# Early expert weights in an attention and mixture-of-experts kernel: five staging buffers, a step moved to the end of a tick, and one matmul group a tick later

## The chip, the cores and the metric

The kernel runs on one core of a Trainium2 chip. The metric is device time in microseconds (us) of one execution; lower is better. Durations of single instructions come from one profiled execution of the kernel before.

## What is computed

Two stages follow each other, and the second needs the first.

```python
# attention: batch 4, heads 8, 768 positions, head size 64, blocks of 32 positions
mask = |block_i - block_j| <= 1, or first or last block, or one of 3 sampled blocks per query block
attn = softmax(where(mask, q @ k.T / 8, -1e9));  x = (attn @ v) as [3072 tokens, 512]
# mixture of experts: 8 experts, hidden size 1024, one expert per token
logits = x @ w_gate + modality_bias[modality_id];  e = argmax(logits);  g = softmax(logits)[e]
out[token] = g * (relu(x @ w1[e]) @ w2[e])
```

## The kernel before, in words

**Attention.** Tokens are handled in 24 tiles of 128. Each half of the batch gives one "dense" tile (first and last block, against all keys) and 11 sparse tiles m = 0 to 10; over both halves the sparse tiles are g = 0 to 21. A sparse tile is four items. For each item the program runs steps named by a letter: S scores (L537), M masked maximum (L545, VectorE), X exponential (L553, ScalarE), T transposes (L562, TensorE), A copy of the transposes out of PSUM (L567, ScalarE); and for each tile W, the product with the values that both query blocks share (`weigh_shared`, L584), V, the product with the values that each has for itself (`weigh_own`, L593), O the division (L447), Y a turn of the tile (L600, L602) and G the gate (L610). The values lie in two buffers, one for even and one for odd g, which are filled anew for each tile: `fetch_v` (L499, L500), `fetch_own` (L525, six transfers of 128 KB), all in the queue of SyncE, and `share_v` (L507, GpSimd), which copies rows from the tile before.

**The order of the work.** It is written out by hand. The loop over ticks t emits in each tick the steps in the order `ORDER` = O X T S M G V A Y W, each for the item that lies `LAG` ticks back, and between them it calls `hook(0)` to `hook(7)`: hook 0 before O, 1 before X, 2 before T, 3 before S, 4 before M, 5 before A, 6 before W, 7 behind all steps. A hook runs the loads put at that place, and by `ADVANCE`, `CHOOSE` and `EARLY` one or more pieces of three generators: the routing of finished tiles, the choosers, and the early groups. There are NI = 104 items; from tick NI on the generators are stepped at the end of each tick, twice in a tick. Every engine's own queue keeps the order in which the program emits.

**The early groups.** `choose(0)` (from 16 finished tiles) and `choose(1)` (from 18) each pick an expert with enough tokens already, so that group 0 and group 1 of 256 tokens can start before attention ends. `choose` multiplies a one-hot matrix on TensorE (L1100, 16 or 18 matmuls of two columns) to get token numbers. `early_groups` (L816) is stepped once per tick. While attention runs, its inner `load(nf, ns)` fetches weight pieces up to nf and splits them up to ns: `fetch` (L712) issues one transfer of 512 KB on SyncE's queue into a staging buffer (`staged`, L709; L720 for pieces of w1, L724 for w2), and `split` (L726) rounds the piece to a high part (a cast on ScalarE, L731) and subtracts to get the low part (L737: on VectorE, or for the pieces in `POOL_SPLITS`, 1, 2, 4 and others, in four parts on GpSimd). The parts go into a ring of NRING buffer pairs `wh`, `wl`. Eight pieces make one expert. `column` (L774, L778, L779) turns the gathered tokens of a group. At the tail (tick NI + 7) the last buffers are set up, and the matmuls of group 0 begin: `up` (L785 to L787), `relu` (L792, L793), `down` (L800 to L802), with `load` calls by the tables `DOWN0`, `UP1`, `DOWN1`.

**Buffers.** SBUF is cut into ten slots, used first by attention and then by the experts (`expert_slots`, L665). Before, the first eight pieces have only two staging buffers in slot 4 (and, for piece 7, one in slot 7, which is free only at the tail), in the order 0, 1, 0, 1, 0, 1, 0, 2; from piece 8 on there are five. The guard in `load` counts with NSTG = 5 all the same, so the transfer of piece 2 is issued when piece 0 is split and has to wait in SyncE's queue until that split has read its buffer. The first tick of the early groups is t = NI - 13, so tick k of `TICKS` is t = NI - 13 + k up to k = 12; ticks 13 and 14 are both at the end of t = NI, 15 and 16 at the end of NI + 1.

**The rest.** From 10 more groups on (`first_layer`, `second_layer`, `later`) the same steps run with LOOK_D = 6 pieces of fetch and LOOK_S = 4 pieces of split ahead.

Of the kernel before, what the change touches and what calls it, by code (L numbers as in the profile page):

```python
# [9 lines left out]
F32 = mybir.dt.float32  # L10
F32R = mybir.dt.float32r
# [51 lines left out]
LHS = (6, 5)  # L63
LHS_DVE = (True, True)
CHOOSE = ((0, 2),)
EARLY = ((3, 3),)

KL = (0, 3)
QP = (-2, 2)
# [10 lines left out]
EVAC_DVE = ()  # L80
POOL_SPLITS = (1, 2, 4, 7, 15, 16, 21)

TICKS = (6, 9, 12)
DOWN0 = ((9, 5), (9, 7), (14, 7), (12, 9), (13, 9), (13, 9), (17, 9), (15, 10))
UP1 = ((13, 8), (13, 14), (17, 15), (20, 15))
DOWN1 = ((16, 17), (17, 16), (17, 17), (23, 18), (21, 17), (23, 18), (23, 19), (22, 19))
# [3 lines left out]
def attention_moe(ctx, tc, kD, qD, qH, v0, v1, blocks, modality, w_gate, bias, w1, w2, out):  # L90
# [33 lines left out]
    with ExitStack() as actx:  # L124
# [5 lines left out]
        def bank():  # L130
            return psum.tile([P, 512], F32, name="bank")


        def slot(n, dt=F32):
            return big.tile([P, 3 * 1024 + (16 if n == 8 else 0)], dt, name="slot", tag=f"slot{n}", bufs=1)
# [521 lines left out]
        stg, wh, wl, xg, xh, xl, hh, hl, og, xq = [], [], [], [], [], [], [], [], [], []  # L657

        def pieces(n, dt, *sizes):
            t, k = slot(n, dt), 0  # L660
            for size in sizes:
                yield t[:, k:k + size]
                k += size

        def expert_slots(*ns):  # L665
            cols_ = lambda ap: ap.rearrange("p (c t) -> p c t", t=GT)
            W, X = 1024, HD
            for n in ns:
                if n == 0:
                    w = [*pieces(1, F32R, W, W, W), *pieces(3, F32R, W, W, W)]  # L670
                    wh[:], wl[:] = w[0::2], w[1::2]
                    wx = list(pieces(9, F32R, W - 16, W, W))[1:]
                    xh.append(cols_(wx[0]))
                    xl.append(cols_(wx[1]))
                    a = list(pieces(4, F32, W, W, X, X))
                    stg.extend(a[0:2])
                    xg.extend(a[2:4])
                elif n == 2:
                    w = [*pieces(0, F32R, W, W, W), *pieces(2, F32R, W)]
                    wh.extend(w[0::2])  # L680
                    wl.extend(w[1::2])
                elif n == 5:
                    a = list(pieces(5, F32R, 2 * W, W))
                    hh.append(cols_(a[0]))
                    hl.append(cols_(a[1]))
                elif n == 6:
                    a = list(pieces(6, F32R, W, W, W))
                    hl.append(cols_(a[0]))
                    xh.append(cols_(a[1]))
                    xl.append(cols_(a[2]))  # L690
                elif n == 7:
                    stg.extend(pieces(7, F32, W, W, W))
                elif n == 8:
                    a = list(pieces(8, F32, X, X, X, X, W))
                    xg.extend(a[0:2])
                    og.extend(a[2:4])
                    xq.append(a[4].rearrange("p (j f) -> p j f", f=P))

        NSTG, NRING, LOOK_D, LOOK_S = 5, 5, 6, 4
        experts = {}  # L700
        out_t = dram_disjoint_views(out, 2)

# [4 lines left out]
            return experts[g]  # L707

        def staged(n):  # L709
            return stg[(0, 1, 0, 1, 0, 1, 0, 2)[n] if n < 8 else n % NSTG]  # L710

        def fetch(n):  # L712
            g, c = divmod(n, 8)
# [12 lines left out]
        def split(n):  # L726
            split_high(n)
            split_low(n, nc.gpsimd if n in POOL_SPLITS else nc.vector)

        def split_high(n):  # L730
            nc.scalar.copy(wh[n % NRING], staged(n))  # L731
# [84 lines left out]
        def early_groups():  # L816
            now = {"fetch": 0, "split": 0, "gather": 0, "column": 0}

            def load(nf, ns):
                while True:  # L820
                    f, p = now["fetch"], now["split"]
                    if p < ns and p < f:
                        split(p)
                        now["split"] += 1
                    elif f < nf and f - NSTG < p and (f < 8 * NEAR or known):
                        fetch(f)
                        now["fetch"] += 1
                    else:
                        return

            def rows(g):
                if now["gather"] == g and ready[g] and (g != 1 or tail[1]):
                    if g == 1:
                        expert_slots(8)
                    gather(g)
                    now["gather"] += 1

            def columns(g):
                for n in range(2):
                    if now["column"] == 2 * g + n and now["gather"] > g:  # L840
                        column(g, n, bank())
                        now["column"] += 1
                        return

            expert_slots(0)
            tick, wait = 0, 0
            while not tail[0]:
                rows(0)
                if now["gather"]:
                    wait += 1  # L850
                    if wait > 4:
                        columns(0)
                p = sum(tick >= x for x in TICKS)
                load(p + 2, p)
                tick += 1
                yield "tick"
            expert_slots(2, 5, 6, 7)
            while now["column"] < 2:
                rows(0)
                columns(0)  # L860
# [186 lines left out]
        def choose(i):  # L1047
            n = TES[i]
# [46 lines left out]
            while any(t < n for t in slots_todo):  # L1095
                yield "tick"
            yield "tick"
            tp = bank()
            for t in range(n):
                nc.tensor.matmul(tp[:, 0:2], lhsT=lhs[:, t, :], rhs=hoh[:, t, :], start=t == 0, stop=t == n - 1)  # L1100
# [120 lines left out]
        def hook(place):  # L1221
            for f in work_at.pop((t, place), []):
                f()
            if t < NI:
# [4 lines left out]
                for at_, k in CHOOSE:  # L1229
                    if place == at_:  # L1230
                        step(choosers, k)
                for at_, k in EARLY:
                    if place == at_:
# [220 lines left out]
```

## Time and profile before

| | |
|---|---|
| device time, median of 3 runs | 520.99 us (517.85 to 523.48) |
| the profiled execution's own time | 519.21 us |
| its span in the trace | 517.4 us |
| mean granted TensorE clock in it | 0.995 of full |
| TensorE busy | 496.7 us, 96% of the span |
| VectorE, ScalarE, GpSimd busy | 389.6, 338.9, 295.1 us |
| moved by DMA | 119.40 MB |

Time outside the span is 519.21 - 517.4 = 1.8 us. PE is TensorE's matmuls, PEld its weight loads, DVE VectorE, ACT ScalarE, POOL GpSimd, SPq the queue of SyncE. Attention runs to about 227 us, and behind it only the experts. A matmul's end is modelled, so a busy PE can hide short stalls; its idle time can't.

### The profile page before, as it was taken

The numbers are of one execution on the slowest core, as the hardware profiler recorded it, in microseconds if no ns is written. First come the engines' busy times: TensorE is split into PE (matmuls) and PEld (weight loads), VectorE is DVE, ScalarE is ACT, GpSimd is POOL, SyncE is SP. The second block draws the span as 40 slices with busy tenths as digits, with TensorE's granted clock in tenths as the row PEclk, the third lists the DMA queues.
The fourth block names the chain that finished last, engine by engine and source line by source line (L and its number), as shares of the span: only waits on it lengthen the run. The fifth ranks groups of instructions, "written<-read, shape, count | busy, mean of one in ns | idle before, by whom it ended". The sixth has DMA issues, their size and how long they took to land.

```text
span 517.4 us, 18858 instructions
## 1 busy us (share of the span) xinstructions
PE 496.7 (96%) x7170; PEld 419.2 (81%) x7170; DVE 389.6 (75%) x1127; ACT 338.9 (66%) x777; POOL 295.1 (57%) x530
## 2 busy tenths in 40 slices
PE   8999989999999989889999999999999999999994
PEld 6677766777777767779989898989989899898983
DVE  7986788677689899866976669586785867759572
ACT  3799877998889988944554456464564546646471
POOL 3579775667458875752457624563845648465410
PEclk9999999999999999899999999999999999999999
DMA  8998788878956787656867875857749567595760
GB/s 281 326 243 232 223 226 250 240 208 249 253 161 186 205 265 224 184 179 243 275 227 252 316 254 158 308 184 264 270 164 333 174 241 249 195 343 157 262 202 23
DMA packets 49698, 119.40 MB, mean 231 GB/s; under 512 B 8512, under 2 KB 8896, under 8 KB 49600
## 3 DMA queue, kind: packets, MB, share of 16 engines
q1 hardware_dynamic: 44656, 105.00, 64.4%
q0 software_dynamic: 4944, 13.11, 7.0%
q8 instruction: 58, 0.95, 0.8%
q14 instruction: 40, 0.33, 0.2%
HBM read 105.50 MB, written 12.85 MB: 229 GB/s over the span
## 4 chain that ended last, share of the span: by engine, by line
PE 35%; POOL 21%; issue 19%; DMA 12%; DVE 6%; SPq 3%; POOLq 2%; ACT 0%; DVEq 0%; ACTq 0%
POOL slot L757 14%; PE bank L537 7%; PE bank L562 6%; DMA out<-slot,si 5%; POOL out L811 5%; PE bank L593 3%; PE bank L584 3%; DMA slot<-v 3%; DMA slot<-w 2%; POOL slot L737 2%; DMA slot<-x_d,gq 2%; PE bank L438 2%; PE bank L610 2%; SPq L525 2%; POOLq L960 1%
## 5 line engine op out<-in xcount | busy, mean ns | idle before, releaser
L737 DVE TENSOR_TENSOR slot<-slot 128x1024 fp32r<-128x1024 f32 x97 | 116.5, 1230 | 42.2 <-ACT slot L731 32.6
L731 ACT CAST slot<-slot 128x1024 fp32r<-128x1024 f32 x104 | 106.2, 1047 | 44.3 <-PE bank L786 18.6
L757 POOL DMA_INDIRECT slot<-x_d,gq x72 | 85.8, 1192 | 76.0 <-DVE slot L764 56.7
L785 PE MATMUL bank<-slot 128*128 128x256 f32 x384 | 107.0, 279 | 0.0
L786 PE MATMUL bank<-slot 128*128 128x256 f32 x384 | 106.2, 277 | 0.0
L787 PE MATMUL bank<-slot 128*128 128x256 f32 x384 | 106.2, 276 | 0.0
L553 ACT ACTIVATE a<-y,mn 128x256 f32<-128x256 f32 x176 | 88.7, 513 | 5.7 <-DVE mn L545 5.6
L802 PE MATMUL bank<-slot 128*128 128x512 f32 x200 | 79.1, 395 | 0.5 <-DVE slot L793 0.5
L800 PE MATMUL bank<-slot 128*128 128x512 f32 x200 | 78.5, 392 | 0.3 <-issue 0.3
L801 PE MATMUL bank<-slot 128*128 128x512 f32 x200 | 78.3, 392 | 0.0
L785 PEld LDWEIGHTS bank<-slot 128*128 128x128 f32 x384 | 72.1, 188 | 0.6
L786 PEld LDWEIGHTS bank<-slot 128*128 128x128 f32 x384 | 72.1, 188 | 0.4
L787 PEld LDWEIGHTS bank<-slot 128*128 128x128 f32 x384 | 72.2, 188 | 0.0
L545 DVE CUSTOM_DVE_ANT_1 y<-bank,smask 128x256 f32<-128x256 f32 x176 | 66.1, 415 | 0.3
L485 POOL COPY slot<-slot 128x128 f32 x264 | 64.5, 295 | 0.0
L507 POOL TENSOR_SCALAR slot<-slot 32x1024 f32<-32x1024 f32 x40 | 41.9, 1047 | 26.2 <-PE bank L593 9.8
L567 ACT COPY at<-bank 128x512 f32<-128x512 f32 x88 | 50.8, 579 | 5.9 <-PE bank L562 5.7
L562 PE MATMUL bank<-ident,a 128*128 128x128 f32 x352 | 52.3, 282 | 0.7 <-DVE mn L545 0.7
L792 ACT ACTIVATE slot<-bank 128x512 fp32r<-128x512 f32 x48 | 26.9, 598 | 37.4 <-PE bank L787 35.4
L811 POOL DMA_INDIRECT out<-slot,si x21 | 28.3, 1348 | 37.0 <-ACT slot L809 23.3
L537 PE MATMUL bank<-slot,q_raw 64*32 64x256 f32 x1408 | 48.9, 382 | 0.0
L793 DVE SCALAR_TENSOR_TENSOR slot<-bank,slot 128x512 fp32r<-128x512 f32 x48 | 30.5, 685 | 24.3 <-ACT slot L792 22.0
(301 smaller groups left out, 880.5 us busy)
## 6 DMA issues: line engine op xcount, KB each, us to landing
slot<-w SPq DMA_DIRECT2D x105, 512.0 KB
slot<-v SPq DMA_DIRECT2D x180, 128.0 KB
q_raw<-qH SPq DMA_DIRECT2D x22, 256.0 KB
x_d<-xr SPq DMA_DIRECT2D x22, 256.0 KB
slot<-v SPq DMA_DIRECT2D x16, 256.0 KB
slot<-kD SPq DMA_DIRECT2D x13, 256.0 KB
slot<-v SPq DMA_DIRECT2D x4, 768.0 KB
slot<-kD SPq DMA_DIRECT2D x3, 768.0 KB
```

Of the source, the lines that this page charges most:

```text
L537: nc.tensor.matmul(sp[u][32 * pr:32 * pr + 32, b * 256:(b + 1) * 256], lhsT=q[r, b * NPAIR + pr, n, :], rhs=kv[r, s0:s0 + 8, b, pr, :], st ...
L553: nc.scalar.activation(a[:, u, :], y[:, u, :], AF.Exp, bias=mn[:, u:u + 1], scale=-1.0, accum_out=total[:, u:u + 1])
L562: nc.tensor.transpose(tp[:, k:k + P], a[:, u, c * P:(c + 1) * P], ident)
L731: nc.scalar.copy(wh[n % NRING], staged(n))
L737: eng.tensor_tensor(l[:, k:k + size], staged(n)[:, k:k + size], h[:, k:k + size].bitcast(F32), ALU.subtract)
L757: nc.gpsimd.indirect_dma_start(out=xq[0][:, 4 * t + k, :], out_offset=None, in_=table, in_offset=bass.IndirectOffsetOnAxis(ap=gq[:, k, 2 * ...
L785: nc.tensor.matmul(o, lhsT=h[:, fs], rhs=xh[g % 2][:, c, :], start=c == 0 and f % 2 == 0, stop=False)
L786: nc.tensor.matmul(o, lhsT=h[:, fs], rhs=xl[g % 2][:, c, :], start=False, stop=False)
L787: nc.tensor.matmul(o, lhsT=l[:, fs], rhs=xh[g % 2][:, c, :], start=False, stop=c == 3 and f % 2 == 1)
L800: nc.tensor.matmul(o, lhsT=hh[0][:, f, ts_], rhs=h[:, fs], start=f == 0, stop=False)
L801: nc.tensor.matmul(o, lhsT=hh[0][:, f, ts_], rhs=l[:, fs], start=False, stop=False)
L802: nc.tensor.matmul(o, lhsT=hl[f // 4][:, f % 4, ts_], rhs=h[:, fs], start=False, stop=f == 7)
```

## The change

It touches five things. The early groups' step moves from hook 3 to hook 7 of each tick before NI. The thresholds for fetches and splits become separate: fetches at ticks 0, 2, 6, 10 and 16, splits still at 6, 9 and 12. The five staging buffers exist from the start (three in slot 0, two in slot 4) and piece n always goes to buffer n % 5. The ring of split weights grows from 5 to 6 pairs, with slots 2 and 7 in place of slot 0 and a part of slot 2. And `choose(1)` waits one more tick ahead of its matmuls.

```diff
-EARLY = ((3, 3),)
+EARLY = ((7, 3),)
...
-TICKS = (6, 9, 12)
+TICKS = ((0, 2, 6, 10, 16), (6, 9, 12))
...
                     a = list(pieces(4, F32, W, W, X, X))
-                    stg.extend(a[0:2])
+                    stg.extend([*pieces(0, F32, W, W, W), *a[0:2]])
                     xg.extend(a[2:4])
                 elif n == 2:
-                    w = [*pieces(0, F32R, W, W, W), *pieces(2, F32R, W)]
+                    w = [*pieces(2, F32R, W, W, W), *pieces(7, F32R, W, W, W)]
...
-                elif n == 7:
-                    stg.extend(pieces(7, F32, W, W, W))
...
-        NSTG, NRING, LOOK_D, LOOK_S = 5, 5, 6, 4
+        NSTG, NRING, LOOK_D, LOOK_S = 5, 6, 6, 4
...
         def staged(n):
-            return stg[(0, 1, 0, 1, 0, 1, 0, 2)[n] if n < 8 else n % NSTG]
+            return stg[n % NSTG]
...
-                p = sum(tick >= x for x in TICKS)
-                load(p + 2, p)
+                load(*(sum(tick >= x for x in ticks) for ticks in TICKS))
                 tick += 1
                 yield "tick"
-            expert_slots(2, 5, 6, 7)
+            expert_slots(2, 5, 6)
...
             while any(t < n for t in slots_todo):
                 yield "tick"
             yield "tick"
+            if i:
+                yield "tick"
             tp = bank()
```

## Rows read from the trace of the kernel before

**Rows 1.** Page, busy time by engine, granted clock in 40 slices, and instruction queue.

```profile
PE 496.7 (96%) x7170; PEld 419.2 (81%) x7170; DVE 389.6 (75%) x1127; ACT 338.9 (66%) x777; POOL 295.1 (57%) x530
...
PEclk9999999999999999899999999999999999999999
...
q8 instruction: 58, 0.95, 0.8%
```

**Rows 2.** Windows: busy time by engine, granted clock, DMA share, GB/s.

```profile
200.00:250.00 50.00, 45.87 (x794) 39.86 (x793) 39.66 (x170) 30.45 (x69) 23.88 (x27) 0.97 0.69 224
...
300.00:350.00 50.00, 50.00 (x339) 45.81 (x338) 37.71 (x41) 27.82 (x35) 25.41 (x19) 1.00 0.70 231
```

**Rows 3.** Waits of PE, 180 to 250 us: total, times, longest.

```profile
PE bank L593 <- DMA slot<-v: 2.0, 1, 2.0
PE bank L584 <- ACT at L567: 1.5, 1, 1.5
PE bank L593 <- issue: 1.1, 1, 1.1
...
PE bank L584 <- POOL slot L507: 0.2, 1, 0.2
```

**Rows 4.** Windows of 1 and 5 us around PE's gaps, columns as in rows 2.

```profile
213.00:214.00 1.00, 0.00 (x0) 0.00 (x0) 0.91 (x3) 1.00 (x2) 0.34 (x1) 1.00 0.88 262
...
216.00:217.00 1.00, 1.00 (x6) 1.00 (x5) 0.09 (x1) 0.55 (x1) 0.91 (x2) 0.50 0.55 164
...
215.00:220.00 5.00, 5.00 (x88) 4.70 (x88) 3.98 (x17) 4.11 (x12) 3.53 (x5) 0.67 0.51 139
...
225.00:226.00 1.00, 0.00 (x0) 0.00 (x0) 0.62 (x5) 1.00 (x2) 0.00 (x0) 1.00 0.27 102
```

**Rows 5.** Timeline of PE: start, us, line, tiles, [idle before <- releaser].

```profile
193.79 0.63 PE L593 MATMUL bank<-slot,at 128*32 128x64 f32 x26 [1.14 <-issue]
...
214.05 1.17 PE L584 MATMUL bank<-slot,at 128*64 128x64 f32 x29 [1.47 <-ACT at L567]
...
220.33 0.60 PE L1100 MATMUL bank<-hoh,lhs 128*128 128x2 f16 x18
...
226.15 1.09 PE L593 MATMUL bank<-slot,at 128*32 128x64 f32 x62 [2.02 <-DMA slot<-v]
```

**Rows 6.** Timeline of SyncE's queue (SPq): when transfers are issued.

```profile
188.05 0.90 SPq L720 DMA_DIRECT2D slot<-w  x2
189.13 3.42 SPq L525 DMA_DIRECT2D slot<-v  x6
...
209.92 0.36 SPq L720 DMA_DIRECT2D slot<-w  x1
...
217.77 0.41 SPq L724 DMA_DIRECT2D slot<-w  x1
218.37 2.82 SPq L525 DMA_DIRECT2D slot<-v  x6
```

**Rows 7.** Waits of SyncE's queue, 184 to 232 us.

```profile
SPq L720 <- POOL slot L737: 2.8, 1, 2.8
```

**Rows 8.** Timeline of ACT around the third early split.

```profile
211.49 0.51 ACT L553 ACTIVATE a<-y,mn 128x256 f32<-128x256 f32 x1
...
212.47 1.05 ACT L731 CAST slot<-slot 128x1024 fp32r<-128x1024 f32 x1
213.41 0.60 ACT L567 COPY at<-bank 128x512 f32<-128x512 f32 x1
214.22 0.51 ACT L553 ACTIVATE a<-y,mn 128x256 f32<-128x256 f32 x1 [0.22 <-DVE mn L545]
```

**Rows 9.** Timeline of POOL: second early split, then the shared values of g = 20.

```profile
207.06 2.83 POOL L737 TENSOR_TENSOR slot<-slot 128x256 fp32r<-128x256 f32 x4 [5.55 <-ACT slot L731]
209.98 2.23 POOL L507 TENSOR_SCALAR slot<-slot 32x1024 f32<-32x1024 f32 x2
```

**Rows 10.** Timeline of DVE: the last step ahead of the second choice's matmuls.

```profile
219.74 0.18 DVE L1090 CAST hoh<-ho 128x36 f16<-128x36 f32 x1
```

## The prediction
> **What bounds the kernel now.** I read the page first: PE is busy 96% of the span and its granted clock is full in all but one of 40 slices [rows 1]. So the question is where PE is idle or slow. Windows by stage answer it: behind attention PE is busy 50.00 of 50 us, while in 200 to 250 us it is busy 45.87, 4.1 less [rows 2]. The place of the change is the end of attention, and what can be won lies there.
>
> The waits of PE name its gaps: 2.0 us for a values transfer, 1.5 us for a copy by ACT, 0.2 us for shared values from POOL, and 1.1 us for nothing that the profile shows [rows 3]. The timeline puts them in order: 1.14 us ahead of 193.79, 1.47 us ahead of 214.05, 2.02 us ahead of 226.15 [rows 5]. From about 212.3 to 214.05 PE runs next to nothing, 1.7 us in all with the wait for POOL. [...]
>
> **The change part by part.** All in us, against the profiled execution (519.21, span 517.4 and 1.8 around it).
>
> *Loads behind values.* Now piece 4 is fetched at tick 12, which is t = NI - 1, ahead of the six value transfers of g = 21 (t = NI and NI + 1). The queue shows it: the weights at 217.77, the six at 218.37 to 221.2 [rows 6]; weigh_own of g = 21 then waits 2.02 [rows 5]. Afterwards piece 4 is fetched at tick 16, the end of NI + 1, behind all six; piece 3 at tick 10 behind those of g = 20; pieces 1 and 2 behind those of their ticks. With five buffers no early transfer waits for a split any more, so SyncE's queue is no longer held, as it was for 2.8 by piece 3 [rows 7]. When do the six land? Their predecessor in the queue, fetch_v of g = 21, overwrites rows that share_v of g = 20 reads; that ends at 209.98 + 2.23 = 212.2 now [rows 9], 212.8 after (below). Six issues at 2.82 in all end near 216.5. The last one now lands 226.1 - 221.2 = 4.9 after its issue with 512 KB ahead of it; even with that it would land at 221.4. PE will ask at 224.1 - 0.95 - 1.65 = 221.5 if the two next terms hold. Gain 2.0, bounds 1.5 and 2.02.
>
> *The step at the end of a tick.* At tick 12 the cast of piece 2 (1.05, at 212.47) stands in front of the copy at 213.41, for which PE's weigh_shared waits until 214.05 [rows 5, 8]. At hook 7 it comes behind the copy, which then runs at 212.47 to 213.07. But at tick 9 the cast of piece 1 slips behind a copy of 0.6 too, and with it the low part on POOL (207.06, now waiting for that cast) and share_v behind it [rows 9]: 212.2 + 0.6 = 212.8, still ahead of 213.07. PE resumes at 213.1 in place of 214.05: gain 0.95; bounds 0 (POOL slips 1.3 further) and 1.47.
> The cast now stands in front of the next exponential instead. That feeds the transposes two ticks later and has slack: after tick 12 the cast ends at 213.07 + 1.05 = 214.12, and the exponential waited for DVE until 214.22 anyway [rows 8]. I take a cost of 0.2 for the other two; bounds 0 and 3 x 1.05 = 3.15, if all three casts come through to PE.
>
> *Clock.* The gap shrinks from 1.7 to some 0.8. The gap of 1.14 ahead of 193.79 was followed by no fall: the page shows one slice below full in the whole span [rows 1, 5]. Gain 1.65, bounds 0 and 1.65.
>
> *Second choice a tick later.* Its 18 matmuls follow weigh_own of g = 20 at the end of NI + 2, at 220.33, when DVE has had their matrix ready since 219.92 [rows 5, 10]. PE comes 0.95 + 1.65 = 2.6 earlier, at 217.7; DVE, which is held by the turned tokens that PE gives it, only 0.95 earlier, at 219.0. In the old place PE would wait 1.3. The added tick puts them behind the transposes of the last item (end of NI + 3), so that these and part of the copy after them fill the wait. I take 0.3; bounds 0 and 1.3. The tokens of group 1 are picked later by as much, but are asked for only behind all of the first `up`, in the middle of `down`; choose's other products are needed later still. No cost there.
>
> *Half the first burst.* Two pieces are fetched together at 188.05 and six values follow [rows 6]; the gap ahead of 193.79 falls into that burst. Afterwards one piece goes ahead of the six and one behind. What ends this gap is not shown, so bounds 0 and 1.14; I take 0.4, since bytes ahead halve, but the same bytes pass before 194.
>
> *Ring of six, other slots.* Splits get a free pair one piece sooner. Behind attention PE has no idle time to give back [rows 2], so 0. Slots 0, 2 and 7 are free in time: their last readers are the first half's keys, the second half's keys and the values of g = 20, all done before the tail. If not, PE would wait at the fourth piece of `up` for the split.
>
> Instructions and bytes are the same in number: 105 weight transfers, the same casts, the same matmuls.
>
> Sum: 2.0 + 0.95 - 0.2 + 1.65 - 0.3 + 0.4 = 4.5. The experts behind it are bound by PE, so all of it reaches the end. 519.21 - 4.5 = 514.7 for the profiled execution. That one lay 1.8 below the median of the runs, so the median goes from 520.99 to 516.5. With every upper bound: 2.02 + 1.47 + 1.65 + 1.14 = 6.3, so 514.7; with every lower one: 1.5 - 1.3 - 3.15 = -2.95, so 523.9.
>
> **Rivals.**
> *The clock falls all the same.* PE still has a gap of some 0.8 there and perhaps a new one at the second choice; and that the 2.02 gap was not followed by a fall while the 1.7 one was speaks for chance in it [rows 4, 5]. Then 4.5 - 1.65 = 2.85 and PE comes 1.65 later, so that the matrix is ready (+0.3): 3.1, and 517.9; with a cast or POOL's slip coming through as well, 2.0 and 519.0. I put it at 518.2.
> [...]
>
> *Hidden anyway.* DVE is busy 39.66 of 50 us in 200 to 250 [rows 2], more in its first half, and the last items' chain of maximum, exponential and copy might set the end of attention whatever PE waits for. For: the exponential at 214.22 waits for DVE [rows 8]. Against: between 214.05 and 224.1 PE has no wait worth a row [rows 3, 5]. Then only 1 of the 4.5 comes through: 520.0.
>
> *Everything goes.* All of the gap ahead of 193.79 and all of the wait for the copy: 6.3, so 514.7.
>
> *Slower: PE's instructions come late.* They come by DMA too: 58 transfers with 0.95 MB, 16.4 KB each [rows 1], one for each 247 of 14,340 instructions; in 200 to 250 that is 1587 / 247 = 6.4 blocks [rows 2]. Pieces 5 to 7 no longer wait for splits at the tail and can be issued some 7 us sooner, 1.5 MB that lie ahead of these blocks. If a late block costs what the unexplained gap cost, 1.14, then four cost 4.6, and with a fall of the clock 6.2: 1.7 slower, 522.7. It decides from three blocks on (3.4 + 1.65 = 5.1 against 4.5). Against: from 300 to 350 the DMA share is as high and PE has no gap [rows 2].
> [...]
>
> **How the numbers follow.** Forecast 0.44 (516.5, itself 515.0 to 518.0), clock falls 0.22, everything goes 0.16, hidden 0.10, slower 0.08. Three runs of the kernel before lie 5.6 apart, so a median of three can be off by 1 or 2; a measurement can tell about 1%, 5.2 us, from no change. The range reaches from somewhat below 514.7 to between hidden and slower: 513.3 to 521.3. Faster by over 1% means under 515.8: nearly all of everything goes and about 0.4 of the forecast, 0.15 + 0.18 = 0.33. Slower by over 1% needs 526.2, worse than the rival's own time: 0.05. The rest is 0.62.
>
> **What would show it.** In SyncE's queue the weights of piece 4 stand behind the six values of g = 21, and no early transfer waits for POOL or ACT. The last weigh_own has no wait for values; the wait of weigh_shared for the copy at g = 20 is under 1. The clock is 1.00 between attention's last scores and the first `up`. That `up` starts near 222.7 in place of 227.2, and from there the two traces differ by a constant. The prediction is wrong if the first `up` starts earlier and the end doesn't (then a wait behind attention is new), if PE waits there for exponentials, DVE or POOL in place of what went, or if gaps for nothing that is shown grow in number.

## The result, and the profile after

| | before | after |
|---|---|---|
| device time, median of 6 runs | 520.25 us (517.47 to 523.48) | 527.93 us (523.53 to 533.42) |
| profiled execution: own time, span | 519.21, 517.4 us | 524.93, 523.2 us |
| mean granted clock | 0.995 | 0.996 |

The ratio is 1.0131, with a 95% interval of 1.0088 to 1.0174: slower by 1.3%, where 0.9% faster was forecast. Medians in us are of all executions, while a ratio, here and below, leaves out those that took over 1.5% longer than the fastest of the same kernel. In the kernel after, lines from L699 on have numbers that are two lower: `up` is L783 to L785, `down` L798 to L800, the cast L729, the column casts L776. The second choice's matmuls (L1100 before) are L1099, the cast of their matrix (L1090) is L1087.

The windows of the kernel after answer to [rows 2]. The columns are the same.

```profile
200.00:250.00 50.00, 45.87 (x801) 39.13 (x800) 41.87 (x172) 31.31 (x71) 24.39 (x27) 1.00 0.78 236
300.00:350.00 50.00, 50.00 (x324) 45.35 (x323) 37.20 (x40) 27.51 (x35) 22.78 (x18) 1.00 0.67 230
```

At the end of attention PE is busy for the same 45.87 us. Behind it PE is busy 50.00 of 50 at full clock, as before, but it runs 324 matmuls where it ran 339. That is the loss, and no busy share and no clock shows it. Only the counts in brackets do.

Waits of PE from 180 to 250 us after the change, against [rows 3]:

```profile
PE bank L785 <- issue: 1.6, 1, 1.6
PE bank L1099 <- DVE hoh L1087: 1.0, 1, 1.0
PE bank L584 <- POOL slot L507: 0.7, 1, 0.7
```

The 2.0 us for the values and the 1.5 us for the copy are gone. A wait of 1.6 us for nothing that the profile shows now stands at the third matmul of the first `up`, and one of 1.0 at the second choice.

Where the 5.8 us of the two spans come from is read from these times on PE: the start of the scores that are just ahead of the change's first transfer, the first `up` of group 0, of group 1 and of group 3 (from where all groups are alike), and the end. First the kernel before, then the kernel after:

```profile
185.47 1.09 PE L537 MATMUL bank<-slot,q_raw 64*32 64x256 f32 x32
...
227.18 0.39 PE L785 MATMUL bank<-slot 128*128 128x256 f32 x1
...
252.54 0.36 PE L785 MATMUL bank<-slot 128*128 128x256 f32 x1
...
301.30 0.28 PE L785 MATMUL bank<-slot 128*128 128x256 f32 x1
```

```profile
187.32 0.66 PE L537 MATMUL bank<-slot,q_raw 64*32 64x256 f32 x15
...
224.27 0.39 PE L783 MATMUL bank<-slot 128*128 128x256 f32 x1
...
251.68 0.36 PE L783 MATMUL bank<-slot 128*128 128x256 f32 x1
...
302.39 0.28 PE L783 MATMUL bank<-slot 128*128 128x256 f32 x1
```

| stretch | before | after | difference |
|---|---|---|---|
| to those scores (the run's own, the change hasn't begun) | 185.47 | 187.32 | +1.85 |
| on to the first `up` (group 0) | 41.71 | 36.95 | -4.76 |
| on to group 1 | 25.36 | 27.41 | +2.05 |
| on to group 3 | 48.76 | 50.71 | +1.95 |
| on to the end of the span | 216.1 | 220.8 | +4.7 |

The sum is 5.8. Up to the first `up` attention gave 4.8, a little more than the 4.5 forecast, but luck has a part in it: 2.3 are two waits for nothing that the profile shows, of 1.13 us at 188.14 and 1.14 us at 193.79, which only the trace before has. Group 0 took 2.05 back, 1.64 of it in the wait at its third matmul, so that 2.7 were left. The rest of the story lies in the two lower rows, where the prediction had put 0.

*The full groups.* The transfers that store a group's output come at a fixed beat. Before, then after:

```profile
345.45 1.00 POOL L811 DMA_INDIRECT out<-slot,si  x1 [0.44 <-ACT slot L809]
...
367.35 1.00 POOL L811 DMA_INDIRECT out<-slot,si  x1 [0.44 <-ACT slot L809]
```

```profile
347.50 1.00 POOL L809 DMA_INDIRECT out<-slot,si  x1 [0.61 <-ACT slot L807]
...
370.13 1.01 POOL L809 DMA_INDIRECT out<-slot,si  x1 [0.59 <-ACT slot L807]
...
392.50 1.00 POOL L809 DMA_INDIRECT out<-slot,si  x1 [0.52 <-ACT slot L807]
...
414.85 1.00 POOL L809 DMA_INDIRECT out<-slot,si  x1 [0.61 <-ACT slot L807]
```

A group takes 21.90 us before. After, it takes 22.63, 22.37 and 22.35, then 22.63 again. That period of three groups is 24 pieces, the least number that both eight pieces and six pairs divide, which points to the ring's pairs. By the distance of their starts, 24 matmuls of `up` take 2.72 us (113.3 ns each) before and in some pieces after, and 2.83 us (117.8 ns) or a little more (up to 122 ns) in the others; those of `down` go from 229 to 233 ns in most pieces. So 4 to 5 ns are lost for most of these matmuls, of either size, and also while ACT and DVE rest (118.0 ns in `up`, where it is 113.3 before).

*The hand-over to group 2.* The queue of ACT, after and then before:

```profile
275.97 1.04 ACT L729 CAST slot<-slot 128x1024 fp32r<-128x1024 f32 x1 [6.68 <-PE bank L799]
276.92 0.58 ACT L776 CAST slot<-bank 128x512 fp32r<-128x512 f32 x1
...
278.35 0.59 ACT L776 CAST slot<-bank 128x512 fp32r<-128x512 f32 x1
```

```profile
273.87 0.59 ACT L778 CAST slot<-bank 128x512 fp32r<-128x512 f32 x1 [3.61 <-PE bank L774]
274.35 1.05 ACT L731 CAST slot<-slot 128x1024 fp32r<-128x1024 f32 x1
275.69 0.59 ACT L778 CAST slot<-bank 128x512 fp32r<-128x512 f32 x1 [0.29 <-PE bank L774]
```

The cast at 275.97 is that of piece 20. In a ring of six it writes the pair of piece 14, not of piece 15, and so it can be ready sooner. The program emits it in `first_layer`, behind the two column casts of group 2, and ACT's queue has it ahead of them. So, against what is said of the kernel before, a queue does not always keep the order in which the program emits: a scheduler orders the queues where the early groups end and the rest begins. That it goes by what is ready sooner is the likely reason, but not shown. It waits 6.68 us for PE to be done with piece 14, and the column casts wait behind it:

```profile
277.55 0.38 PE L783 MATMUL bank<-slot 128*128 128x256 f32 x1 [0.94 <-ACT slot L776]
278.93 0.39 PE L784 MATMUL bank<-slot 128*128 128x256 f32 x1 [0.99 <-DVE slot L777]
```

These two waits, 1.93 us together, are about the 1.95 us. Runs 5 and 7 test it.

### The profile page after: what moved, and what is told of

Same layout as the page of the kernel before. It is cut to its first block, busy times and chain, and to the rows that moved or that the text cites. A ratio compares the mean times of both kernels' runs of the same rounds, so it can differ in the third digit from the quotient of the medians.

```text
span 523.2 us, 18863 instructions
## 1 busy us (share of the span) xinstructions
PE 502.2 (96%) x7170; PEld 422.3 (81%) x7170; DVE 394.3 (75%) x1127; ACT 337.5 (65%) x777; POOL 295.5 (56%) x530
## 4 chain that ended last, share of the span: by engine, by line
PE 71%; DVE 9%; DMA 8%; ACT 5%; issue 4%; SPq 1%; POOL 1%; POOLq 0%; DVEq 0%; ACTq 0%
PE bank L783 8%; PE bank L784 8%; PE bank L785 8%; PE bank L798 7%; PE bank L800 7%; PE bank L799 7%; PE bank L537 6%; DMA out<-slot,si 6%; PE bank L562 5%; PE bank L584 3%; PE bank L593 3%; ACT a L553 2%; PE bank L610 2%; PE bank L438 1%; DVE y L545 1%
## 5 line engine op out<-in xcount | busy, mean ns | idle before, releaser
L755 POOL DMA_INDIRECT slot<-x_d,gq x72 | 88.9, 1235 | 80.1 <-DVE slot L762 60.8
L729 ACT CAST slot<-slot 128x1024 fp32r<-128x1024 f32 x104 | 104.2, 1048 | 22.2 <-DMA slot<-w 8.0
L785 PE MATMUL bank<-slot 128*128 128x256 f32 x384 | 107.8, 281 | 1.6 <-issue 1.6
L783 PE MATMUL bank<-slot 128*128 128x256 f32 x384 | 108.5, 283 | 0.9 <-ACT slot L776 0.9
L784 PE MATMUL bank<-slot 128*128 128x256 f32 x384 | 108.0, 281 | 1.0 <-DVE slot L777 1.0
L798 PE MATMUL bank<-slot 128*128 128x512 f32 x200 | 79.7, 399 | 0.0
L800 PE MATMUL bank<-slot 128*128 128x512 f32 x200 | 79.1, 395 | 0.0
L783 PEld LDWEIGHTS bank<-slot 128*128 128x128 f32 x384 | 72.6, 189 | 1.6 <-ACT slot L776 1.1
L785 PEld LDWEIGHTS bank<-slot 128*128 128x128 f32 x384 | 72.3, 188 | 1.8 <-issue 1.8
L790 ACT ACTIVATE slot<-bank 128x512 fp32r<-128x512 f32 x48 | 28.6, 599 | 67.6 <-PE bank L785 53.0
L791 DVE SCALAR_TENSOR_TENSOR slot<-bank,slot 128x512 fp32r<-128x512 f32 x48 | 32.7, 691 | 49.9 <-ACT slot L790 45.3
L537 PE MATMUL bank<-slot,q_raw 64*32 64x256 f32 x1408 | 50.0, 382 | 0.2 <-ACT at L567 0.2
L809 POOL DMA_INDIRECT out<-slot,si x21 | 25.4, 1211 | 38.0 <-ACT slot L807 24.3
```

The costliest lines, as they stand in the source:

```text
L537: nc.tensor.matmul(sp[u][32 * pr:32 * pr + 32, b * 256:(b + 1) * 256], lhsT=q[r, b * NPAIR + pr, n, :], rhs=kv[r, s0:s0 + 8, b, pr, :], st ...
L755: nc.gpsimd.indirect_dma_start(out=xq[0][:, 4 * t + k, :], out_offset=None, in_=table, in_offset=bass.IndirectOffsetOnAxis(ap=gq[:, k, 2 * ...
L783: nc.tensor.matmul(o, lhsT=h[:, fs], rhs=xh[g % 2][:, c, :], start=c == 0 and f % 2 == 0, stop=False)
L784: nc.tensor.matmul(o, lhsT=h[:, fs], rhs=xl[g % 2][:, c, :], start=False, stop=False)
L785: nc.tensor.matmul(o, lhsT=l[:, fs], rhs=xh[g % 2][:, c, :], start=False, stop=c == 3 and f % 2 == 1)
L798: nc.tensor.matmul(o, lhsT=hh[0][:, f, ts_], rhs=h[:, fs], start=f == 0, stop=False)
```

## The experiments

Runs without a ratio are one execution each. The time of one kernel differs by several us from execution to execution (517.47 to 523.48 for the kernel before), so they are read by stretches of their traces and not by their times.

Theory A for the full groups starts from the addresses. Slots 0 to 3 and 9 lie behind 64 bytes of padding, so in the kernel before every weights' piece is 64 bytes out of step (modulo 128 and modulo 1024) with the tokens and the hidden values that it is multiplied with. The sixth pair, and half of the fifth, lie in slot 7 after the change, ahead of the padding and in step with them.

**1. The padding in front of the pieces in slot 7**

```diff
-return big.tile([P, 3 * 1024 + (16 if n == 8 else 0)], ...)
+return big.tile([P, 3 * 1024 + (16 if n == 7 else 0)], ...)
...
-w = [..., *pieces(7, F32R, W, W, W)]
+w = [..., *list(pieces(7, F32R, 16, W, W, W))[1:]]
```

> The kernel after with one edit: the 64 bytes of padding stand in front of the ring's three pieces in slot 7 and no longer behind slot 8, so the fourth and fifth pairs' pieces lie 64 bytes further on and slots 0 to 3 and 9 stay where they were. Theory A (a matmul is slower when the weights' piece has the same address, modulo 128 bytes, as the tokens' or the hidden operand): a full group comes down from the 22.45 us of the kernel after to the 21.89 us of the kernel before, a 256-column matmul from 117.7 to 113.3 ns, and the whole to about 520 us (524.9 less 5.0). Theory B (a ring of six pairs is slower in itself, by the order of the splits): group stays at 22.45 us, whole at 525 to 528. Theory C (the chip's condition in that run): also without regard to the edit; the kernel before, on the same chip, then says what it had.

Measured: 519.43 us (the kernel before 521.49 on that chip), group 21.89 us. The first matmuls of `up` and `down` from 324 to 500 us by form (mean ns behind the bar), in the kernel after and in this one:

```profile
L783 PE MATMUL bank<-slot 128*128 128x256 f32 x256 | 71.8, 281 | 0.0
...
L798 PE MATMUL bank<-slot 128*128 128x512 f32 x123 | 48.8, 397 | 0.0
```

```profile
L783 PE MATMUL bank<-slot 128*128 128x256 f32 x256 | 70.8, 276 | 0.0
...
L798 PE MATMUL bank<-slot 128*128 128x512 f32 x128 | 49.7, 388 | 0.0
```

A shift of 64 bytes gave the whole rate back, with the ring still at six. The eight later traces with this padding (runs 5, 6 and 11 to 16) have groups of 21.89 too. The hand-over took 52.1 us from group 1 to group 3: the two waits stayed (1.0 each), and here the clock fell behind them, to 0.61 and 0.54 of full in 278 to 282 us.

**2. Ring of five on the new slots**

```diff
-NSTG, NRING, LOOK_D, LOOK_S = 5, 6, 6, 4
+NSTG, NRING, LOOK_D, LOOK_S = 5, 5, 6, 4
```

> The kernel after with five pairs in the ring instead of six; one piece of the five (the low part of the fifth pair) is still in slot 7, without padding. Theory A (address of the weights' piece against the other operand): slower matmuls only where the fifth pair is read, so a group of 21.9 to 22.4 us, with slow pieces once in five. Theory B (six pairs in themselves): all groups back at 21.89 us. Theory D (the output banks moved by one with the new order of the early groups): 22.45 us as in the kernel after.

Measured: 523.33 us. The stores of the groups:

```profile
326.29 1.75 POOL L809 DMA_INDIRECT out<-slot,si  x1 [0.30 <-issue]
348.61 1.75 POOL L809 DMA_INDIRECT out<-slot,si  x1 [0.30 <-issue]
370.54 1.75 POOL L809 DMA_INDIRECT out<-slot,si  x1 [0.30 <-issue]
392.96 1.74 POOL L809 DMA_INDIRECT out<-slot,si  x1 [0.30 <-issue]
415.16 1.74 POOL L809 DMA_INDIRECT out<-slot,si  x1 [0.30 <-issue]
```

Groups of 22.32, 21.93, 22.42 and 22.20 us: with one piece of five in step the loss comes and goes, as A has it and B and D do not. From group 1 to group 3 it takes 48.5 us with no wait: in a ring of five piece 20 can't be cast early.

**3. The kernel before with a sixth pair in slot 2, behind the padding**

```diff
-w = [*pieces(0, F32R, W, W, W), *pieces(2, F32R, W)]
+w = [*pieces(0, F32R, W, W, W), *pieces(2, F32R, W, W, W)]
...
-NSTG, NRING, LOOK_D, LOOK_S = 5, 5, 6, 4
+NSTG, NRING, LOOK_D, LOOK_S = 5, 6, 6, 4
```

> The kernel before with six pairs in the ring, the sixth in the two unused pieces of slot 2 (slot 7 stays with the staging). Theory A: nothing slower, group 21.89 us, whole 519 to 521 us. Theory B (six pairs in themselves): group about 22.45 us, whole about 525 us.

Measured: 527.54 us, group 22.31. This goes against A: no piece is in step, and `up` is slower all the same (117.8 ns), in every group from the fourth (group 3) on, while `down` all but keeps its rate (229 ns) and the third group's `up` still has 113.3 ns in its second to fourth piece. The hand-over has the two waits of the kernel after:

```profile
PE bank L786 <- DVE slot L779: 1.0, 1, 1.0
PE bank L785 <- ACT slot L778: 0.9, 1, 0.9
```

**4. The kernel before with everything in step**

```diff
-return big.tile([P, 3 * 1024 + (16 if n == 8 else 0)], ...)
+return big.tile([P, 3 * 1024], ...)
...
-wx = list(pieces(9, F32R, W - 16, W, W))[1:]
+wx = list(pieces(9, F32R, W, W, W))[1:]
```

> The kernel before without the 64 bytes of padding behind slot 8 and without the 16 elements left out at the start of slot 9: weights' pieces and the other operands then have the same address modulo 128 bytes everywhere. Theory A: every expert matmul is slower, a 256-column matmul at 117 ns or more, group 22.4 us or more, whole 526 us or more (9 or 10 groups by 0.56). Theories B, C and D: group 21.89 us, whole as the kernel before.

Measured: 528.51 us, group 22.42; `up` at 120 ns in every group, `down` at 227, a little faster than the usual 229. So in the kernel before a change of the addresses alone brought the loss, 22.42 us a group in place of 21.90. But the third run, with 22.31 us and no piece in step, shows that they are not all.

**5 and 6. The cast of piece 20 put behind the column casts, on top of the padding; and the same with the change's three edits of order undone**

```diff
-load(22, 20)
+load(22, 21)
...
-if n + look < 8 * NGMAX:
+if n + look < 8 * NGMAX and (do_, n + look) != (split, 20):
```

> The kernel of the first experiment (padding in front of the ring's pieces in slot 7) with one more edit: the split of piece 20 is issued in the early groups, behind the third group's column casts, and no longer in the first layer of the third group, from where the order of the engines' queues had put its cast ahead of the column casts. Theory (the loss at the hand-over between the second and third group comes from that cast): the stretch from the first up of the second group to the first up of the fourth falls from the 52.1 us of the first experiment to 48.5 to 49 us, as in the kernel before, with no wait of 0.9 us or more on the column casts and no fall of the clock behind it; full groups stay at 21.89 us; whole 515 to 517 us, 0.985 to 0.995 of the kernel before. Rival (the six pairs cost there in another way): the stretch stays above 50 us and the whole at 519 us.

> The kernel of the run ahead of it with the three changes of order undone (early groups' step after the third place of a tick, loads at the old ticks, second choice multiplied without the extra tick); ring of six, padding, five staging buffers and the split of piece 20 stay. By the prediction's terms (2.0 for the loads, 1.0 for the step less 0.2, 1.65 for the clock, 0.3 less for the choice) it is some 3 us slower than the run ahead of it, 518 to 520 us. Rival (what the order gives in attention is lost again before the experts): as fast as the run ahead of it, within 1 us.

Measured: 521.31 us, ratio 1.0028 (0.9984 to 1.0072), and 523.71 us, ratio 1.0078 (1.0038 to 1.0118). The hand-over theory holds: 48.5 us from group 1 to group 3, no wait on a column cast, groups of 21.89. The three edits of order are worth 2.4 us by the medians, near the 3 expected, though the two intervals overlap. Run 6 is slower than the kernel before, with an interval clear of 1, although neither the rate nor the hand-over costs anything in it: its group 0 takes 31.6 us, with a wait of 2.8 us at the third `up`. In run 5, too, the whole is 5 us over the expectation: from group 0 to group 1 it takes 31.5 us where the kernel before takes 25.4. In the fifth run's trace PE waits 2.6 us at the third `up`, and the clock falls behind that (granted clock: the third number from the end):

```profile
224.00:228.00 4.00, 1.41 (x24) 1.11 (x13) 3.84 (x14) 2.50 (x3) 1.75 (x2) 1.00 0.90 333
228.00:232.00 4.00, 4.00 (x33) 3.84 (x32) 1.14 (x7) 0.00 (x0) 3.54 (x5) 0.56 0.70 218
232.00:236.00 4.00, 4.00 (x24) 4.00 (x22) 0.69 (x1) 1.09 (x2) 0.22 (x1) 0.58 0.85 314
```

**7. The third kernel with the cast of piece 20 behind the column casts** (the edit of run 5 on run 3)

> The kernel before with six pairs in the ring as in the third experiment, and the split of piece 20 behind the column casts. Theory (that cast makes the loss at the hand-over): from the first up of the second group to the first up of the fourth 48.5 to 49 us instead of 51.5. On the group's time two theories: history (the rate of the up matmuls is a state that PE carries on from the hand-over, with the same operands): 21.89 us where the hand-over is the one of the kernel before; addresses alone (the sixth pair's pieces decide): 22.31 us as in the third experiment.

Measured: 519.53 us, 48.2 us from group 1 to group 3, group 21.89. The operands, their addresses and PE's whole program are those of run 3, and `up` has 113.3 ns. So the same operands ran at either rate, and the rate behind the hand-over held for the groups that followed, 117.8 ns in run 3 from group 3 on and 113.3 here. The two runs were on different chips, but single traces show the same. Groups 2 and 8 read and write the same buffers in the same order in a ring of six. In run 3 `up` has 113.3 ns in group 2 (second to fourth piece) and 117.7 in group 8, and in run 5 it is the other way round, 117.7 in group 2 and 113.3 in group 8. In run 3 the last matmul of `down` is followed by the first `up` after 227 ns, and `up` stays at 117.8; here it is 231 and in the kernel before 230 to 231, and after five matmuls `up` is at 113.3. This agrees with the history theory; a state of PE itself is in no trace.

**8. A small matmul between the layers of run 3**

```diff
 def first_layer(g):
+    nc.tensor.matmul(hp[0][:, 0:16], lhsT=ident, rhs=gf[:, 0:16], start=True, stop=True)
```

> The kernel of the third experiment (before with six pairs, group 22.31 us, up matmuls at 117.7 ns) with one small matmul (16 columns, fp32, into the first output bank, whose result the first up matmul overwrites) ahead of each group's first up. History (the rate is a state handed from one matmul to the next, which a break between the layers sets anew): the ups run at 113.3 ns in some or all groups, group 21.9 to 22.1 us with the small matmul in it. Addresses alone: ups stay at 117.7 ns, group 22.4 us.

Measured: 522.51 us, group 22.11 with 0.2 us of small matmul in it. By form, run 3 and then this run:

```profile
L786 PE MATMUL bank<-slot 128*128 128x256 f32 x256 | 71.9, 281 | 0.0
```

```profile
L786 PE MATMUL bank<-slot 128*128 128x256 f32 x256 | 70.7, 276 | 0.0
...
L922 PE MATMUL bank<-gf,ident 128*128 128x16 f32 x16 | 2.3, 221 | 0.0
```

From group 3 on `up` has the faster rate behind the small matmul. It need not: in group 2 of this run, behind the same small matmul and the two waits of the hand-over, `up` stayed at 117.7 ns. With runs 1, 3, 4 and 7 this is what was measured of the main loss: with operands in step `up` ran at 120 ns in every group (run 4) and, with a pair and a half of the ring in step, at 117.8 to 122 ns in most pieces (the kernel after); with all of them out of step it ran at 113.3 ns in the kernel before and in runs 1 and 7, and at 117.8 in run 3. What decides between the two rates out of step, no run shows.

**9 and 10. Parts of the change alone, on the kernel before: the step and the second choice; and the second fetch moved off the first's tick**

```diff
-EARLY = ((3, 3),)
+EARLY = ((7, 3),)
...
+            if i:
+                yield "tick"
             tp = bank()
```

Run 10 has in addition:

```diff
-TICKS = (6, 9, 12)
+TICKS = ((0, 2, 6, 9, 12), (6, 9, 12))
```

> The kernel before with two parts of the change alone: the early groups' step at a tick's end and the second choice multiplied a tick later; ring, slots, staging and loads are those of the kernel before. By the prediction's terms (1.0 less 0.2 for the step, 1.65 if the clock stays up, 0.3 for the choice) it is 1 to 3 us faster than the kernel before, 517 to 519 us, ratio 0.994 to 0.998. Rival (hidden anyway): ratio 1.000 within the interval. In its trace the full groups stay at 21.89 us and no wait on column casts of 0.9 us stands at the hand-over, since the ring has five pairs.

> The run ahead of it with the loads of the weights given ticks of their own too, as far as two staging buffers allow: the second piece is fetched at tick 2 and no longer at tick 0 together with the first. By the prediction's term for the first burst (half of a gap of 1.1 us, at most the 2.0 us of all loads) 0.4 to 1 us faster than the run ahead of it; rival: the same within 0.5 us.

Measured: 520.38 us, ratio 1.0036 (0.9999 to 1.0072), and 522.13 us, 1.0018 (0.9972 to 1.0064). No gain is measured, so the rival holds for these parts by themselves, and the two runs can't be told apart. In run 9 the wait of `weigh_shared` is down from 1.47 to 0.74 us, but the 1.7 us for values at the last `weigh_own` are still there. In run 10's trace they are 1.9, and PE waits another 3.1 us for queries (`q_raw`) at 207 us, so this run says little about the first burst.

**11 and 16. Run 5 with the fetches of pieces 5 to 9 in the middle of the first `up`**, timed twice

```diff
-load(10, 5)
+load(5, 5)
 for k in range(4):
+    if k == 2:
+        load(10, 5)
```

> The fifth kernel (change with padding and with the split of piece 20 behind the column casts) with the fetches of pieces 5 to 9 issued after half of the first expert's up matmuls, behind the tokens' writes, and no longer at the end of attention. Theory (the wait of 0.8 to 2.8 us at the first group's third up matmul, which stands in all five traces with five staging buffers and in none with the old staging, and the fall of the clock behind it, come from that burst of four loads at 219.7 us, which keeps the DMA engines at 0.9 to 1.06 just as PE enters the experts' code): no wait there above 0.5 us, clock 1.00 in 224:240, group 0 back from 31.5 to 25 to 26 us, median 4 to 5 us under the fifth kernel's, 516 to 518 us, ratio to the kernel before 0.990 to 0.997. Rival (the wait is PE's own at that place, whatever the DMA engines do): wait of 1 to 3 us again and the median at 521 us.

> The same kernel as e11, timed again. If its gain is real, the ratio to the kernel before is 0.993 to 0.998 again; rival (chance): 1.000 or above.

Measured: 517.17 us, ratio 0.9972 (0.9938 to 1.0005); the second time 519.56 us, 1.0003 (0.9963 to 1.0044). In run 11's trace the clock is 1.00 in 200 to 244 and group 0 takes 27.4 us, but the wait at the third `up` is there again with 1.6 us, so the burst doesn't make it. In run 16's trace, of the same kernel, the wait isn't there. The second timing takes back the gain over the kernel before.

**12 to 15. What the wait at the third `up` belongs to.** Eight small matmuls (two instructions each) ahead of the first `up` in runs 12 and 14, one in runs 13 and 15, on run 11:

```diff
 o = bank()
+for _ in range(0 if k else 8):
+    nc.tensor.matmul(o[:, 0:16], lhsT=ident, rhs=ident[:, 0:16], start=True, stop=True)
```

> The kernel of the run ahead of it with eight small matmuls (16 columns, fp32, into the bank whose first up matmul overwrites them) ahead of the first group's first up, which move that up eight matmuls on in PE's program. The wait stood ahead of the third up matmul, the 5263rd matmul of PE, in all six traces with five staging buffers. Theory (PE's instructions come late at that place of its program): the wait of 0.8 to 2.8 us now stands ahead of the third small matmul, and none stands ahead of the third up. Rival (the up itself waits, for its low weights or its address): the wait stays ahead of the third up matmul, behind all eight small ones.

> As the run ahead of it, with one small matmul (two instructions, 0.23 us) in place of eight. Theory (place of PE's program): a wait of 0.8 to 2.8 us ahead of the first up matmul, which is now the 5263rd. Theory (the third up itself, or a point in time that it must reach): the wait ahead of the third up matmul again. A run in which no wait stands anywhere would say that the small matmul's position alone, or chance, removes it.

> The same kernel as e12 (padding, split of piece 20 behind the column casts, late fetches, eight small matmuls of 1.8 us together ahead of the first up), now timed. If the wait at the third up is always covered by them: 1.8 us of matmuls in place of a wait of 1.6 us, so the same as e11 within 1 us, 516.5 to 518 us, ratio to the kernel before 0.994 to 0.999; if PE's going on there also saves falls of the clock, 514.5 to 516.5 us, ratio 0.991 to 0.995.

> The same kernel as e13 (padding, split of piece 20 behind the column casts, late fetches, one small matmul ahead of the first up). If the gain in attention is real and the wait at the edge of PE's block of instructions is a matter of the run, 516 to 518 us, ratio to the kernel before 0.993 to 0.998, the same as e11 within 1 us. If the small matmul does away with that wait in every run, 514 to 516 us, ratio 0.989 to 0.994. Rival (no gain left): ratio 1.000.

Measured: run 12 517.47 us and run 13 514.82 us, neither with a wait there. Run 14 has 523.46 us (six of its twelve executions took over 524) and a ratio of 0.9999 (0.9950 to 1.0049), run 15 518.28 us, 0.9968 (0.9926 to 1.0010). In these two the wait stands, and it has moved. Run 14:

```profile
227.78 0.72 PE L593 MATMUL bank<-slot,at 128*32 128x64 f32 x37
228.44 0.40 PE L864 MATMUL bank<-ident 128*128 128x16 f32 x2
229.77 1.74 PE L864 MATMUL bank<-ident 128*128 128x16 f32 x14 [0.94 <-issue]
231.35 0.36 PE L783 MATMUL bank<-slot 128*128 128x256 f32 x1
```

Two small instructions, a wait, then the other 14 and the `up` matmuls without one. In run 15 it stands ahead of the first `up` (1.24 us). In both, 5262 matmuls have run ahead of it, as in the kernel after. So it belongs to a place of PE's program. Counting the matmuls ahead of PE's unexplained waits of 0.5 us or more gives, in the last part of attention, the same few places in all traces:

```
matmuls ahead   wait in us (run)
4379            1.13 (before), 0.84 (3, 12), 0.54 to 0.56 (5, 8, 9)
4506            1.14 (before)
4632            2.92 (3), 0.60 (8)
4759            1.31 (5), 0.67 (6), 0.98 (7), 0.89 (11), 2.00 (12), 1.01 (14), 0.58 (15)
5011            0.77 (5), 1.46 (6), 0.94 (11), 0.93 (13), 1.98 (14), 1.31 (15)
5262            1.64 (after), 0.75 (1), 2.19 (2), 2.59 (5), 2.80 (6), 1.59 (11), 0.94 (14), 1.24 (15)
```

They are 126 or 127 apart, or about twice that, and such waits earlier in attention (at 846 to 1855, from 20 us on) stand on the same step. Seven stand off it: 1.34 (8) and 0.54 (9) at 5196, two matmuls ahead of the wait for the values, and five of 0.50 to 0.55 at 4691 to 4694. A matmul and its weight load are two instructions (7170 of each in the kernel before [rows 1]), so this is a step of 252, near the one transfer of 16.4 KB per 247 instructions that the prediction worked out [rows 1]. The traces hold these transfers too (queue q8, 16,384 bytes each). Ahead of each of the 59 waits that stand on the step, in the 18 traces, one of them landed 1.2 to 1.8 us before PE went on, where they come some 5 us apart. So these waits are read, here and below, as PE waiting at the edge of a block of its instructions for the next block; that PE had run out of instructions is not itself in the traces.

At place 5262 the block landed at 224.52 us before and at 224.99 after. What differs is when PE wants it: from place 5137 it took 6.15 us before, 2.02 of them in the wait for the values, and 3.72 us after. A wait of 0.5 us or more stands at this place in 8 of the 11 traces with five staging buffers, where the values no longer hold PE up, and in none of the 7 with the old staging.

No run with the losses taken out is measurably faster than the kernel before. The best are runs 11 and 15, with intervals that hold 1.

## Why the prediction was wrong, point by point

**The step that failed** is the one on the ring and the slots: "Behind attention PE has no idle time to give back, so 0". It asked only whether PE would have to wait, and took 50.00 busy of 50 for a rate that can't change. The ring cost 4.7 us by PE's rate (runs 1, 4, 7, 8) and 1.95 by the order of ACT's queue (runs 2, 5, 7). With it fell "all of it reaches the end", for which the 1.64 us at the third `up` is a second reason. The padding was in the code to be seen, and so was the move of three pieces of the ring, one pair and a half, ahead of it. The sum for attention itself, 4.5 against 4.8 up to the first `up`, came out, in part by luck.

**Loads behind values** (2.0): half of the argument is right, and the gain is not kept. After, the weights stand behind the six values, and the wait at the last `weigh_own` is gone:

```profile
214.87 3.93 SPq L525 DMA_DIRECT2D slot<-v  x6
...
219.93 2.21 SPq L722 DMA_DIRECT2D slot<-w  x4
```

But in run 6, with the old ticks, a weights' transfer stands ahead of the six values again:

```profile
214.46 0.50 SPq L722 DMA_DIRECT2D slot<-w  x1
215.15 2.82 SPq L525 DMA_DIRECT2D slot<-v  x6
```

PE doesn't wait for them there either. All seven traces with the old staging have the wait (0.7 to 2.0 us), and none of the eleven with five buffers has it. So the order of the fetches isn't needed to remove it; the five buffers do it, with which SyncE's queue no longer waits for a split ahead of the first `up` (2.8 and 1.5 us in 184 to 222 before, none after), as the prediction says too. And PE comes 64 matmuls further and waits at the edge of a block, 1.6 us in this trace and 0 to 2.8 in the others with five buffers. While PE waited for values in the trace before, up to 226.15, the block came in, at 224.52. Even in the trace before, the 2.0 would not have been kept whole: with PE going on 1.4 us after the block lands, as in the trace after, at 225.9, and PE at the place by 227.52 - 2.02 = 225.5, some 0.4 would have been lost again (an estimate).

**The step at a tick's end** (0.95 less 0.2): nearly right. The wait ahead of `weigh_shared` went from 1.47 to 0.74 us, a gain of 0.73, and it now ends on the shared values of POOL, which the prediction had ready just in time.

**Clock** (1.65): no run shows this term by itself. It is 5 x (1 - 0.67), by the clock granted in 215 to 220 before [rows 4], an estimate. What the runs show in its place is the granted clock. The forecast of it is right in this trace, 1.00 in 200 to 250 in place of 0.97 [rows 2]. It isn't a gain for good: near the end of attention the clock fell to 0.50 behind the waits of 2.19, 2.59 and 2.80 us in runs 2 (228 to 232), 5 and 6 (230 to 234 in both), and to 0.61 and 0.54 at the hand-over in run 1.

**Second choice** (0.3 lost): mis-sized. PE waits 1.0 us for the matrix in the kernel after, 0.4 in runs 1 and 5.

**Half the first burst** (0.4): not told apart. The 1.14 us ahead of 193.79 [rows 5] stand at place 4506, and the block landed 1.6 us before PE went on, so they are read as a wait for instructions. The block's transfer took 0.9 us, where others take up to 2.2, so the burst didn't slow the transfer; why it didn't start sooner isn't shown. The 1.14 us are absent after, and in other runs of either order too. The trace before has another such wait, at place 4379, which the prediction passed over:

```profile
188.14 0.29 PE L610 MATMUL bank<-wg_raw,xT 128*64 128x8 f32 x5 [1.13 <-issue]
```

**The rivals.** The slower one had the right thing in view, late blocks of instructions, and its price for one (1.14) is of the size of the waits found. It is not what decided: waits put down to "issue" add up to 2.6 us in the kernel before and 2.1 after within 180 to 260. Nor does it need the burst of pieces 5 to 7, as run 11 shows. The prediction weighed it down by the stretch from 300 to 350, where PE has no gap [rows 2]. Few blocks are waited for by 0.5 us or more, 59 in 18 traces with 58 or 59 blocks each. But in attention one of these waits took up to 2.92 us (run 3), and the gap of 1.14 stands at such an edge too, place 4506. The warning sign that the text names, a first `up` that starts earlier while the end doesn't, came true.

## What to carry to other kernels

A buffer that moves keeps its size and dates but not its address: when a kernel has padding of a few bytes, find out what it keeps out of step before new buffers go ahead of it. Where an engine is busy all the time, compare the number of instructions in a window and the distance of their starts, not the busy share. And when a buffer comes free sooner, look at what the scheduler now puts first in each engine's queue. A wait taken away can also uncover the next one: here PE, no longer held for 2.02 us by values, waited 1.64 us at what is read as the edge of a block of its instructions.

## What the runs showed of the hardware

- The rate of back-to-back matmuls differed with where the two operands lie to each other. Matmuls of 256 columns started 113.3 ns apart with all pieces 64 bytes out of step (run 1, the kernel before), 117.8 to 122 ns apart in most pieces of the kernel after, where a pair and a half of the ring is in step, and 120 ns apart with everything in step (run 4), all behind attention, where the granted clock is 1.00 in 300 to 350 before and after. By which power of two the addresses are compared wasn't tried.
- The same operands had both rates. With the same addresses, order and program of PE, `up` ran at 117.8 ns from group 3 on in run 3 and at 113.3 in run 7. With one small matmul ahead of each group, the second matmuls of `up` in 324 to 500 us have a mean of 276 ns by form (run 8), where run 3 has 281.
- Of the waits of 0.5 us or more that the profile puts down to "issue" in attention and at the first `up`, 59 stand at places of PE's program that are 126 or 127 matmuls apart, or a multiple of that, and seven stand elsewhere. The wait at one place differs by the run, as at place 5262: 1.64 us in the kernel after, 2.80 in run 6, none of 0.5 us or more in the kernel before. At each of the 59 a 16,384-byte transfer of the instruction queue landed 1.2 to 1.8 us before PE went on (18 traces).
- Two waits of 1 us each were followed by a granted clock of 0.61 and 0.54 in run 1 (278 to 282 us) and of 1.00 in the kernel after (277.5 to 302.5); one of 2.6 us by 0.56 and 0.58 in run 5 (228 to 236), one of 1.6 us by 1.00 in run 11 (228 to 244).
